# Taking two heads in one transpose: a regrouped second batch in an attention and feed-forward kernel

## The chip, the cores and the metric

One core of one Trainium2 chip runs the whole program. The metric is the device time of one execution in microseconds (us). Executions of one kernel differ by about 1%, so a kernel is given as the median of several runs with the lowest and the highest, and two kernels are compared by a ratio with a 95% interval. A run over 1.5% above the fastest of its kernel is called slow and left out of the ratio (five runs of the kernel before in all the rounds below, none of another). TensorE is the matmul engine, VectorE, ScalarE and GpSimd the others.

## The reference

```python
# q, k, v: (8 batches, 12 heads, 448 positions, 64); the weights: 768 x 1536 twice, 1536 x 768
scores = q @ k.T / sqrt(64)
attn   = relu(scores) ** 2 / 448
x      = (attn @ v)                    # regrouped to 3584 x 768
out    = (gelu(x @ w_gate) * (x @ w_val)) @ w_out
```

## The kernel before

A planner in Python lays all instructions in order: each piece of work has a place in time, and the pieces are interleaved on TensorE by their places. Nearly every matmul uses one quarter of the array, 64 rows by 64 columns. `row` and `col` name the quarter. Four matmuls on four quarters run at the same time, and a product of full width is a pair on one half of the rows (two column halves) and a pair on the other half.

```python
def mm(o, lhsT, rhs, row, col, start, stop):
    return nc.tensor.matmul(o, lhsT, rhs, start=start, stop=stop,
                            tile_position=(P * row, P * col))          # P = 64
```

Scores need q and k with the head dimension on the partitions, so both are transposed first. A batch has three groups (`m`) of four heads. The first two batches (`EARLY = 2`) are transposed on TensorE, one head at a time; later ones by DMA, from a copy `qkr` in which VectorE has put the heads of a group side by side.

```python
def add_transposes(at, b, m, rs):          # batches 0 and 1
    def emit(i, n, c):                     # i: q (upper partitions) or k (lower)
        ...
        src = qk16[b].rearrange("p (h c d) -> p h c d", c=SC, d=D)
        for j in range(2):                 # one head each
            nc.tensor.transpose(
                t[HALF[j], n, c * P:(c + 1) * P], src[HALF[i], 2 * (2 * m + rs[n]) + j, c, :],
                ident[HALF[i], HALF[i]], tile_position=(P * i, P * j))
    ...
    both(at, zip(*ops), GS / 2 if b else 0.0)

def add_dma_transposes(b, m):              # batches 2 to 7
    wait = Op("IDLE", 2.0, lambda: None,
              [head_op[b, pr, i] for pr in (2 * m, 2 * m + 1) for i in range(2)])
    def emit_copy():
        ...
        nc.vector.tensor_copy(
            qkr[b][:, m], qk16[b].rearrange("p (h c d) -> p c h d", c=SC, d=D)[:, :, 4 * m:4 * m + 4])
```

The last line of `add_transposes` matters most below: for the second batch (b = 1, counted from 0) each small step of transposes is put half a matmul step (`GS / 2`) after the last, so a group is not one run but is spread among the other matmuls. These are the gate and value products `x @ w_gate` and `x @ w_val`, which appear in the profile as `ff<-xT,wg` and `ff<-xT,wv`.

## Time and profile before

| what | before |
|---|---|
| time, 6 runs beside the changed kernel | 432.66 us median (431.25 to 435.29) |
| profiled run, span and mean granted clock | 432.1 us, 0.993 |
| two batches in the steady part | 99.1 us |
| fetch stop at 50.9 us, half clock after it | 1.94 us, 3.41 us |
| wait for the VectorE product at 96.65 us | 1.58 us |

The prediction shows the page's head and the stretches around the dips. These two stretches ahead of the first dip are used later; the columns are the stretch, its length, then TensorE, weight loads, VectorE, ScalarE and GpSimd (busy time and count each), the granted clock, the DMA share and GB/s.

```profile
30.00:40.00 10.00, 9.59 (x244) 8.76 (x243) 5.20 (x9) 6.00 (x8) 6.00 (x8) 1.00 1.39 198
40.00:50.00 10.00, 10.00 (x244) 8.08 (x239) 6.58 (x12) 6.80 (x9) 4.92 (x7) 1.00 1.45 197
```

About 244 matmuls start in each ten microseconds, at full clock.

This is TensorE's timeline of the kernel before, in the middle of a spread group: start, duration, line and operation, and how many records the line stands for.

```profile
49.30 0.22 PE L333 MATMUL sp<-ident,qk 64*64 64x64 bf16 x4
49.35 0.35 PE L159 MATMUL ff<-xT,wv 64*64 64x448 bf16 x2
49.42 0.35 PE L159 MATMUL ff<-xT,wg 64*64 64x448 bf16 x2
49.55 0.22 PE L333 MATMUL sp<-ident,qk 64*64 64x64 bf16 x4
```

Between two sets of four small transposes stand a pair on each half of the rows, 0.07 us apart, and the next transposes come 0.13 us after the second pair. The ends of matmuls are modelled: one lasts 0.35 us here, though a new set of four starts every 0.19 us. What counts is the distance between starts. The small transposes slip in at almost no cost.

A group of the page of the kernel before: busy time, mean ns of one, then the idle time of the engine just before them and what ended most of it.

```profile
L258 DVE COPY qkr<-qk 128x1792 bf16<-128x1792 bf16 x18 | 19.4, 1080 | 3.3 <-DMA qkT<-qkr 2.3
```

The 18 copies of L258 serve the six later batches, and 2.3 us of the idle time before them is a wait for the DMA transposes that still read the buffer.

### The profile page before, as it was taken

What the parts mean: (1) busy time and instruction counts of PE and PEld (TensorE: products, weight loads), DVE (VectorE), ACT (ScalarE), POOL (GpSimd) and SP (SyncE); (2) the same over time, 40 slices, a digit from 0 to 9 for tenths busy, and PEclk for the clock granted to TensorE, in tenths of its full rate; (3) what the DMA queues carried; (4) which work ended last, traced back from release to release, by engine and by line L of the source; (5) the groups of instructions that cost most, each with busy time, mean ns of one, the idle gap of its engine ahead of it and who ended that gap; (6) DMA issues with size and microseconds to landing.
All of it is one profiled execution on the core that took longest, in us unless ns stands there. A gap on an engine that the chain in (4) does not pass through costs nothing.

```text
span 432.1 us, 19964 instructions
## 1 busy us (share of the span) xinstructions
PE 419.5 (97%) x9279; PEld 361.3 (84%) x9279; DVE 212.0 (49%) x345; ACT 224.9 (52%) x323; POOL 71.6 (17%) x117
## 2 busy tenths in 40 slices
PE   8899899989999999999999999999999999999995
PEld 4568668867899888979999978979999988977895
DVE  3866556358543675356633675346643555212200
ACT  4856554266666555565556555555546555322221
POOL 7655320023000230013200231012200000000000
PEclk9999989999999999999999999999999999999998
DMA  7999999899533899259913699258912100220024
GB/s 98 193 200 197 201 209 177 144 146 168 81 76 77 99 143 96 76 90 136 146 39 90 95 150 115 77 80 130 161 39 77 39 4 2 45 70 3 3 76 111
DMA packets 75378, 44.92 MB, mean 104 GB/s; under 512 B 36128, under 2 KB 71840, under 8 KB 75296
## 3 DMA queue, kind: packets, MB, share of 16 engines
q0 software_dynamic: 37088, 24.39, 43.7%
q1 hardware_dynamic: 37968, 19.08, 25.0%
q8 instruction: 72, 1.18, 1.1%
q10 hardware_dynamic: 240, 0.20, 0.2%
q14 instruction: 10, 0.08, 0.1%
HBM read 48.76 MB, written 11.01 MB: 138 GB/s over the span
## 4 chain that ended last, share of the span: by engine, by line
PE 89%; DMA 3%; DVE 3%; issue 1%; ACT 1%; POOL 1%; ACTq 0%; SPq 0%; DVEq 0%; POOLq 0%
PE ff L159 82%; PE sp L159 7%; DMA qkT<-qkr 2%; DMA qk<-in_k_dram 2%; DVE attnT L393 1%; DVE qkT L339 1%; ACT rl L387 1%; POOL qk L211 1%; PE sp L333 1%; DVE xT L443 0%; DVE uT L487 0%; ACT osb L538 0%; ACTq L543 0%; PE ff L333 0%; SPq L262 0%
## 5 line engine op out<-in xcount | busy, mean ns | idle before, releaser
L159 PE MATMUL ff<-xT,wg 64*64 64x448 bf16 x2304 | 219.9, 351 | 1.9 <-issue 1.9
L159 PE MATMUL ff<-xT,wv 64*64 64x448 bf16 x2304 | 219.3, 351 | 1.6 <-DVE uT L487 1.6
L387 ACT ACTIVATE rl<-sp 128x896 bf16<-128x896 f32 x168 | 152.2, 919 | 104.5 <-PE sp L159 84.1
L159 PE MATMUL ff<-wo,uT 64*64 64x384 bf16 (+1 forms) x2736 | 150.6, 320 | 0.0
L159 PEld LDWEIGHTS <-wv 64*64 64x64 bf16 x2304 | 126.6, 107 | 18.9 <-issue 3.6
L159 PEld LDWEIGHTS <-wg 64*64 64x64 bf16 x2304 | 126.7, 107 | 18.8 <-issue 3.5
L393 DVE TENSOR_TENSOR attnT<-rl 128x896 bf16<-128x896 bf16 x168 | 103.8, 622 | 75.1 <-ACT rl L387 73.4
L159 PEld LDWEIGHTS <-uT 64*64 64x64 bf16 x2736 | 127.4, 107 | 4.1
L159 PE MATMUL sp<-qkT 64*64 64x448 bf16 (+1 forms) x768 | 107.6, 329 | 0.9 <-ACT rl L387 0.9
L487 DVE TENSOR_TENSOR uT<-gel,ff 128x448 bf16<-128x448 bf16 x96 | 59.5, 620 | 74.2 <-PE ff L159 64.0
L159 PE MATMUL ff<-attnT,v 64*64 64x448 bf16 (+1 forms) x768 | 85.5, 326 | 0.4 <-DVE attnT L393 0.4
L482 ACT ACTIVATE gel<-ff 128x448 bf16<-128x448 f32 x96 | 52.1, 543 | 49.5 <-PE ff L159 48.3
L538 ACT COPY osb<-ff 128x384 f32<-128x384 f32 (+1 forms) x57 | 26.9, 471 | 49.4 <-PE ff L159 46.2
L159 PEld LDWEIGHTS <-qkT 64*64 64x64 bf16 x768 | 44.0, 107 | 8.9 <-issue 3.3
L159 PEld LDWEIGHTS <-v 64*64 64x64 bf16 x768 | 45.6, 107 | 5.0 <-issue 0.5
L443 DVE TENSOR_SCALAR xT<-ff 128x448 bf16<-128x448 f32 x48 | 29.9, 623 | 32.2 <-PE ff L159 31.5
L211 POOL DMA_DIRECT2D qk<-in_q_dram x25 | 15.5, 622 | 156.5 <-DVE uT L487 149.5
L224 POOL DMA_DIRECT2D v<-in_v_dram x44 | 27.3, 628 | 35.1 <-DVE uT L487 25.4
L211 POOL DMA_DIRECT2D qk<-in_k_dram x25 | 15.4, 615 | 39.9 <-DVE uT L487 27.7
L258 DVE COPY qkr<-qk 128x1792 bf16<-128x1792 bf16 x18 | 19.4, 1080 | 3.3 <-DMA qkT<-qkr 2.3
L333 PEld LDWEIGHTS <-qk 64*64 64x64 bf16 x336 | 8.9, 112 | 4.8 <-issue 2.3
L339 DVE COPY qkT<-ff 128x448 bf16<-128x448 bf16 (+1 forms) x8 | 3.9, 503 | 6.8 <-PE ff L333 6.8
(22 smaller groups left out, 46.1 us busy)
## 6 DMA issues: line engine op xcount, KB each, us to landing
out_dram<-osb SPq DMA_DIRECT2D x54, 192.0 KB, 2.7
v<-in_v_dram POOLq DMA_DIRECT2D x42, 128.0 KB, 6.6
qk<-in_q_dram POOLq DMA_DIRECT2D x23, 224.0 KB, 5.3
qk<-in_k_dram POOLq DMA_DIRECT2D x23, 224.0 KB, 5.4
wg<-in_moe_w_gate_dram POOLq DMA_DIRECT2D x6, 384.0 KB, 10.4
wv<-in_moe_w_val_dram POOLq DMA_DIRECT2D x6, 384.0 KB, 11.4
wo<-in_moe_w_out_dram POOLq DMA_DIRECT2D x4, 576.0 KB, 15.3
v<-in_v_dram POOLq DMA_DIRECT2D x2, 384.0 KB, 10.5
```

The source lines that it names most:

```text
L159: return nc.tensor.matmul(o, lhsT, rhs, start=start, stop=stop, tile_position=(P * row, P * col))
L211: op = load(4 * (h1 - h0) * S * D, lambda: nc.gpsimd.dma_start(tile_of().rearrange("p (h x) -> p h x", h=H)[:, h0:h1, :], src[b, h0:h1].re ...
L224: return nc.gpsimd.dma_start(v16[b][HALF[i], h0:h1, :, :], v[b, h0:h1].rearrange("h (p c) d -> p h c d", c=SC)[:, :, c0:c0 + VC, :])
L258: nc.vector.tensor_copy(qkr[b][:, m], qk16[b].rearrange("p (h c d) -> p c h d", c=SC, d=D)[:, :, 4 * m:4 * m + 4])
L333: nc.tensor.transpose(t[HALF[j], n, c * P:(c + 1) * P], src[HALF[i], 2 * (2 * m + rs[n]) + j, c, :], ident[HALF[i], HALF[i]], tile_positio ...
L339: nc.vector.tensor_copy(dst[:, rs[0]:rs[-1] + 1, :, HALF[i]], box[i].rearrange("d r (c p) -> d r c p", c=SC))
L387: nc.scalar.activation(rl[:, :, :], box[0][:, :, 0:S], AF.Relu)
L393: nc.vector.tensor_tensor(a[:, :, :], box[1][:, :, :], box[1][:, :, :], op=ALU.mult)
L443: nc.vector.tensor_scalar_mul(xT[b][:, pr, :], box[0][:, 0:S], scalar1=out_scale)
L482: nc.scalar.activation(gel[b, fc][:, :], box[0][:, 0:S], AF.Gelu)
L487: u_op[b, fc].ins = nc.vector.tensor_tensor(uT[b][:, fc, :], gel.pop((b, fc))[:, :], box[0][:, 0:S], op=ALU.mult).ins
L538: nc.scalar.copy(ob[:, cols], box[0][:, 0:N])
```

## The change

The intent is to halve the number of transposes in the second batch. VectorE first puts its heads side by side, as it does for later batches, and one transpose then takes two heads, 64 rows by 128 columns of the array. Besides, the second pair of heads of the first group of batch 0 is transposed later, the first group of the second batch is placed 3 us of planned time later, fillers stop at 30 us of planned time instead of 64, and from batch 3 on the planned copy waits 5.0 us instead of 2.0 after its loads.

```diff
-    FILL = 64.0
+    FILL = 30.0
...
-    def add_dma_transposes(b, m):
+    def add_relayout(b, m):
-        wait = Op("IDLE", 2.0, lambda: None,
+        wait = Op("IDLE", 2.0 if b <= EARLY else 5.0, lambda: None,
...
+        copy = Op("DVE", 0.65, emit_copy, [wait, *tr_op.get((b - 1, m), ())], lag=0.15, prio=3)
+        DVE.append(copy)
+        return copy
...
             t = box[i]
+            if b:
+                nc.tensor.transpose(
+                    t[:, n, c * P:(c + 1) * P],
+                    qkr[b][HALF[i], m, c, 2 * rs[n]:2 * rs[n] + 2, :].rearrange("p h d -> p (h d)"),
+                    ident[HALF[i], HALF[i]], tile_position=(P * i, 0))
+                return
...
+        copy = add_relayout(b, m) if b else None
         for i in range(2):
-            have = [*(head_op[b, 2 * m + r, i] for r in rs), *(units[-SB:1 - SB] if b else ring_dep())]
+            have = [*(head_op[b, 2 * m + r, i] for r in rs), copy, *(units[-SB:1 - SB] if b else ring_dep())]
...
+            tr_op[b, m] = [ops[0][-1], ops[1][-1]]
...
-                    work.append((lo + SC * m * step - (5.0 if b else 3.0), 1, add_transposes, (b, m, rs)))
+                    x = 1.5 * step if rs == (1,) else (-5.0 if m else -2.0) if b else -3.0
+                    work.append((lo + SC * m * step + x, 1, add_transposes, (b, m, rs)))
```

More of the change, by code (lines that the diff above doesn't have):

```diff
@@ L259, in emit_copy, with add_dma_transposes @@
                 qkr[b][:, m], qk16[b].rearrange("p (h c d) -> p c h d", c=SC, d=D)[:, :, 4 * m:4 * m + 4])
+        copy = Op("DVE", 0.65, emit_copy, [wait, *tr_op.get((b - 1, m), ())], lag=0.15, prio=3)
+        DVE.append(copy)
+        return copy
+    def add_dma_transposes(b, m):
         def emit_transpose(c0, c1):
@@ L264, in emit_transpose @@
                 qkr[b][:, m, c0:c1].rearrange("p c h d -> p (c h d)"))
-        copy = Op("DVE", 0.65, emit_copy, [wait, *tr_op.get((b - 1, m), ())], lag=0.15, prio=3)
-        DVE.append(copy)
+        copy = add_relayout(b, m)
         tr_op[b, m] = [Op("SP", 0.19 * 2 * (c1 - c0), lambda c0=c0, c1=c1: emit_transpose(c0, c1),
```

## The prediction

> **What bounds the kernel now.** I read the page first.
>
> ```profile
> span 432.1 us, 19964 instructions
> ...
> PE 419.5 (97%) x9279; PEld 361.3 (84%) x9279; DVE 212.0 (49%) x345; ACT 224.9 (52%) x323; POOL 71.6 (17%) x117
> ...
> q8 instruction: 72, 1.18, 1.1%
> ```
>
> TensorE is busy for 97% of the span, every other engine for about half, so only what TensorE waits for or executes counts. Then I read busy time by stretch, over the whole span and again around each dip.
>
> ```profile
> 50.00:60.00 10.00, 7.68 (x144) 4.81 (x138) 4.44 (x9) 3.85 (x6) 2.48 (x5) 0.83 1.22 208
> 60.00:70.00 10.00, 10.00 (x227) 7.75 (x222) 6.71 (x12) 7.10 (x10) 1.64 (x3) 1.00 1.23 206
> ...
> 90.00:100.00 10.00, 8.42 (x187) 6.65 (x183) 6.58 (x10) 5.69 (x9) 1.83 (x3) 1.00 0.88 127
> ...
> 130.00:180.00 50.00, 50.00 (x1117) 44.09 (x1114) 27.03 (x44) 29.00 (x41) 7.33 (x12) 1.00 0.79 98
> ```
>
> The columns are length, then TensorE, weight loads, VectorE, ScalarE, GpSimd, granted clock, DMA share, GB/s. From 100 us to 380 us TensorE is busy 10 of 10 at full clock; the change has nothing to win there. Before that, after the start-up of 28 us (where ScalarE and VectorE take turns and TensorE runs fillers), there are just two dips: near 51 us, with a lowered clock, and near 95 us.
>
> ```profile
> 50.90:52.80 1.90, 0.00 (x0) 0.00 (x0) 0.00 (x0) 0.25 (x1) 0.61 (x1) 1.00 1.34 203
> 52.80:54.10 1.30, 1.01 (x20) 0.43 (x21) 0.57 (x1) 0.61 (x1) 0.02 (x1) 1.00 1.18 209
> 54.10:57.50 3.40, 3.29 (x38) 2.02 (x41) 1.83 (x4) 1.06 (x2) 1.20 (x2) 0.50 1.16 211
> ```
>
> The first dip: 1.94 us with no TensorE instruction, 0.4 us waiting for a copy, then 3.4 us at a clock of 0.50, which costs 3.4 x 0.5 = 1.7 us more. Together 4.0 us. In time order:
>
> ```profile
> 50.49 0.11 PEld L159 LDWEIGHTS <-wv 64*64 64x64 bf16 x2
> 50.52 0.36 PE L159 MATMUL ff<-xT,wv 64*64 64x448 bf16 x2
> ...
> 52.81 0.11 PEld L159 LDWEIGHTS <-wg 64*64 64x64 bf16 x2 [2.21 <-issue]
> 52.81 0.38 PE L159 MATMUL ff<-xT,wg 64*64 64x448 bf16 x2 [1.94 <-issue]
> ```
>
> "issue" means that nothing the profile shows held TensorE: VectorE had been idle since 50.78. I think it ran out of instructions. The instruction queue moved 72 packets, 1.18 MB, so 16 KB each; TensorE has 2 x 9279 rows, about 72 packets of 256. Putting the queue's DMA records beside TensorE's records, a fetch starts some time after TensorE enters a block of 256 and must land before it ends. The row after the stop is row 1985 = 193 + 7 x 256, on a boundary. That fetch started at 50.35, 3.7 us after TensorE entered the block at 46.62, and landed at 51.30; TensorE went on 1.51 us later. Four blocks between 16 and 47 us show similar times from landing to the next block (1.40 to 1.64), and 4.6 to 4.8 us from entry to landing in four of the five between 22 and 57. So while the weights stream in (DMA share above 1.2), 256 instructions can't be had faster than every 4.7 + 1.45 = 6.1 us. A block of full-width matmuls takes that anyway (0.189 us per 8 rows, 32 x 0.189 = 6.05). The block at 46.62 held 48 of the short transposes and only 4 us of work.
>
> The second dip:
>
> ```profile
> 94.99 1.08 DVE L258 COPY qkr<-qk 128x1792 bf16<-128x1792 bf16 x1 [2.26 <-DMA qkT<-qkr]
> ...
> 95.99 0.61 DVE L487 TENSOR_TENSOR uT<-gel,ff 128x448 bf16<-128x448 bf16 x1
> ...
> 96.65 0.38 PE L159 MATMUL ff<-xT,wv 64*64 64x448 bf16 x4 [1.58 <-DVE uT L487]
> ```
>
> VectorE reached the first regrouping copy of batch 3, whose single buffer was still being read by the last DMA transpose of batch 2, and the product behind it, which frees TensorE's bank, came late: 1.58 us lost.
>
> **What the Trainium skill says.** "Runtime: NRT & Kernel Launch", Instruction fetch mechanics, has blocks of 16 KiB (256 instructions), the next fetched while the current runs; the trace agrees on size, but not that it is hidden. "DMA: Bandwidth & Descriptors", Queues, rings and completion order, has each DMA engine go round the rows at packet granularity, which fits a fetch delayed 3.7 us at 203 GB/s. "TensorE: Matmul & The Clock Gate", What's actually happening, halves the clock after an idle window of about 3.4 us; here 1.94 us (2.3 us of the ten) was followed by 3.4 us at half clock, while the 1.11 us stop before 11.88 was not. "TensorEngine Tiling (Array Packing)", Key Properties: "Mode switching requires drain". The trace agrees for one switch, 64x64 to 128x128 and back:
>
> ```profile
> 9.41 0.39 PE L159 MATMUL sp<-qkT 64*64 64x224 bf16 x8
> 9.73 0.50 PE L296 MATMUL ff<-warm 128*128 128x256 bf16 x3
> 10.17 0.38 PE L159 MATMUL sp<-qkT 64*64 64x448 bf16 x4
> 10.49 0.28 PE L296 MATMUL ff<-warm 128*128 128x256 bf16 x1
> ```
>
> Three fillers span 0.50 us and one lasts 0.28, so they are 0.11 apart and the last starts at 9.95; the score follows 0.22 later instead of 0.11. The next switch, scores to filler, takes 10.49 - 10.17 = 0.32 where two steps of scores overlap by 0.19. Each switch costs about 0.1 us. That drain is the danger in this change.
>
> **The change part by part.** The order of both programs shows the rest.
>
> 1. Transposes of batch 1: 168 of 64x64 become 84 of 64x128, 168 TensorE rows fewer (7 more fillers, 154 fewer in all). Between neighbours' starts, dense small ones took 0.013 to 0.019 us each, 0.7 to 0.9 us per group of 56. If the big ones stream alike, 3 x 0.4 = 1.2 us are saved.
> 2. Block boundaries shift. Counting at 0.0473 us per full matmul (0.189 / 4), the blocks after the start hold 5.6, 5.4, 5.6, 5.2 and 5.9 us of work: every one is near 6.1, so instead of one stop of 1.94 I expect stops of 0.4 to 0.9, too short to lower the clock. From 30 us: 36.1, 42, 48.1, 54.2, then 102 rows (2.35 us) to the place that TensorE passed at 60.7 before: 56.5. Gain 4.2 us (3.7 to 4.6).
> 3. Three more VectorE copies, 3 x 1.08 = 3.2 us. The later two lie in idle time of VectorE, and their loads land (32.4 and 39.8 us by the semaphores) before the copies' turns near 34.7 and 41.9. The first stands before the fifth xT copy, at about 26.9, but two qkT copies (0.6 each) move behind it: xT is as early as before. Cost about 0.
> 4. Batch 0's first scores precede the second pair's transposes: 0.1 to 0.2 us of a ScalarE-bound start.
> 5. Regrouping from batch 3 on stands one gate-value step (about 2.5 us) later on VectorE, and the last batch 2 transposes are queued partly ahead of the output stores. The 1.58 us go. Later batches have no TensorE idle time to lose or win.
>
> Without a drain: 4.2 + 1.6 + 0.1 = 5.9 us, 431.3 - 5.9 = 425.4.
>
> **The rivals.** (a) 64x128 is another tiling mode than 64x64, and the new transposes stand among 64x64 matmuls in 38 separate runs: 38 x 2 x 0.1 = 7.6 us of drains, of which about 1 us is hidden in the first group, which waits for xT anyway. Blocks grow to 6.7, 7.5, 6.1 and 8.0 us, the fetch stops vanish, and the same place comes at 61.7: 1.0 us lost there, 1.6 won at 95 us, so about 430.7. For it: fillers do drain. Against it: rows stay split in the same halves, only columns merge. (b) Half a drain each (0.05): about 428. (c) Fetches stay late and one stop exceeds 2 us, so that the clock falls again: 2 us lost from the best case, 427.5. (d) The new first copy delays xT and the score behind it: up to 1 us, 426.4.
>
> **Range and chances.** I give 0.4 to no drain, 0.35 to a full one, 0.25 to between: 0.4 x 425.4 + 0.35 x 430.7 + 0.25 x 428 = 427.9; I say 427.5. 2% faster needs 422.7, more than the two dips together, so 0.05. Slower by 2% (439.9) would need drains twice as costly: 0.02.
>
> **What would show it.** Transposes from qkr: their starts to the next 64x64 matmul at about 0.03 us (no drain) or 0.1 and more (drain). The stop near 51 us: gone or below 1 us, clock 1.00 there. Around 90 to 95 us: no wait of TensorE for uT, no wait of the regrouping copy for the DMA transpose. From 100 us on: 10 of 10, the same 99.1 us per two batches. I am wrong if the steady part changes, if a stop of 2 us stays, or if the start-up before 28 us moves by over 1 us.

## The result

| | before | after |
|---|---|---|
| median of 6 runs | 432.66 us (431.25 to 435.29) | 446.61 us (442.79 to 447.71) |
| profiled run: span, mean granted clock | 432.1 us, 0.993 | 445.9 us, 0.975 |

The ratio is 1.0295, with a 95% interval of 1.0238 to 1.0352. A ratio here is the mean time of one kernel's fast runs over that of the other's fast runs of the same rounds, so it is not quite the ratio of the medians. The changed kernel is slower, and the prediction of 427.5 us, faster than before, was wrong.

The head of the page of the changed kernel, with the clock in tenths of full speed for 40 slices of 11.1 us:

```profile
span 445.9 us, 19815 instructions
...
PE 438.2 (98%) x9202; PEld 361.2 (81%) x9202; DVE 215.0 (48%) x348; ACT 225.0 (50%) x323; POOL 71.6 (16%) x117
...
PEclk9988598999999999999999999999999999999999
```

TensorE executes 77 matmuls fewer and is "busy" 18.7 us longer. The clock line says where to look: the third to seventh slices. The same stretches as before:

```profile
30.00:40.00 10.00, 9.78 (x125) 5.02 (x127) 4.14 (x7) 2.89 (x5) 5.95 (x8) 0.66 1.40 198
40.00:50.00 10.00, 10.00 (x100) 4.06 (x96) 3.06 (x6) 3.10 (x4) 4.90 (x8) 0.73 1.45 197
50.00:60.00 10.00, 10.00 (x164) 5.90 (x164) 6.63 (x11) 4.65 (x6) 2.67 (x5) 0.75 1.21 209
60.00:70.00 10.00, 10.00 (x128) 5.00 (x124) 3.81 (x7) 3.73 (x5) 1.50 (x2) 0.93 1.24 204
...
90.00:100.00 10.00, 10.00 (x229) 8.64 (x223) 2.24 (x3) 2.45 (x5) 0.62 (x1) 1.00 1.16 153
130.00:180.00 50.00, 50.00 (x1126) 44.54 (x1121) 27.14 (x44) 29.70 (x42) 7.32 (x12) 1.00 0.66 95
```

Read the counts, not the busy time. From 40 to 50 us TensorE is busy 10.00 of 10.00 in both kernels, but 100 matmuls start instead of 244, and the weight loads are busy 4.06 us instead of 8.08. A busy stretch is an unbroken chain of matmul durations here, and it says nothing of how much of the array works. The granted clock is 0.66 to 0.93 in these stretches. From 90 us on the clock is full and the counts are those of full work.

One of the stretches at half clock by itself, in the view of stretches of the changed kernel:

```profile
44.68:54.92 10.24, 10.24 (x95) 4.36 (x97) 4.03 (x6) 2.92 (x4) 4.76 (x7) 0.50 1.36 201
```

There are three such stretches: 31.03 to 37.86 (6.83 us), 44.68 to 54.92 (10.24) and 68.58 to 71.99 (3.41), which is 20.48 us in all. At half speed they lose 20.48 x 0.5 = 10.24 us. Before there was one of 3.41 us, which lost 1.71. So 10.24 - 1.71 = 8.5 us of the loss is clock alone.

To see the rest I counted only the matmuls that both kernels share (no transposes, no fillers), took the n-th of each, and subtracted the clock's loss so far. The changed kernel is then behind as follows:

| part of the program (time before, us) | behind without the clock, us | step |
|---|---|---|
| start to 27 | about 0 | |
| first group of transposes, to 29 | 1.7 | +1.7 |
| second group, to 37 | 4.8 | +3.1 |
| third group, most of it, to 50 | 7.6 | +2.8 |
| rest of the third group, past the fetch stop of before, 60 to 93 | 6.2 | -1.4 (+0.9 and -2.3) |
| past the wait of before at 96.65 | 4.5 | -1.7 |
| past small fetch stops of after, from 116 on | 5.3 | +0.8 |

The sum is 5.3 + 8.5 = 13.8 us, which is the difference between the two traces from 130 us to the end (13.78 to 13.84).

What a group looks like now, in the timeline of the changed kernel:

```profile
30.16 0.38 PE L159 MATMUL ff<-xT,wg 64*64 64x448 bf16 x2
30.47 0.29 PE L336 MATMUL sp<-ident,qkr 64*128 64x64 bf16 x6
30.69 0.38 PE L159 MATMUL ff<-xT,wg 64*64 64x448 bf16 x2
31.00 0.34 PE L336 MATMUL sp<-ident,qkr 64*128 64x64 bf16 x5
31.27 0.58 PE L159 MATMUL ff<-xT,wg 64*64 64x448 bf16 x2
```

A pair of 64x64 matmuls starts at 30.16, and the next transpose only 0.31 us later, although the pair streams its 448 columns in 0.19 us. After a single transpose the next pair starts 0.13 us later (30.03 to 30.16 just ahead of these lines). Between two sets of transposes there is now only one pair, on one half of the rows: the other half has nothing. The last duration, 0.58 us, is already at half clock.

What the prediction had expected of VectorE did happen. The group of regrouping copies, and the whole list of TensorE's waits from 20 to 100 us, in the changed kernel:

```profile
L258 DVE COPY qkr<-qk 128x1792 bf16<-128x1792 bf16 x21 | 22.6, 1078 | 0.0
```

```profile
PE sp L159 <- ACT rl L399: 0.6, 2, 0.4
PE sp L336 <- DVE qkT L349: 0.2, 1, 0.2
```

In the kernel before that list was headed by these two:

```profile
PE ff L159 <- issue: 1.9, 1, 1.9
PE ff L159 <- DVE uT L487: 1.6, 1, 1.6
```

The columns are the total, the number and the longest. Both dips are gone. A list of waits does not show the new loss at all, since it is time in which TensorE counts as busy.

### The profile page after: what moved, and what is told of

Its sections match the earlier page's. It is cut to its first block, busy times and chain, and to the rows that moved or that the text cites. A ratio compares the mean times of both kernels' runs of the same rounds, so it can differ in the third digit from the quotient of the medians.

```text
span 445.9 us, 19815 instructions
## 1 busy us (share of the span) xinstructions
PE 438.2 (98%) x9202; PEld 361.2 (81%) x9202; DVE 215.0 (48%) x348; ACT 225.0 (50%) x323; POOL 71.6 (16%) x117
## 4 chain that ended last, share of the span: by engine, by line
PE 93%; DVE 2%; DMA 1%; ACT 1%; POOL 1%; issue 1%; ACTq 0%; POOLq 0%
PE ff L159 84%; PE sp L159 7%; PE sp L336 2%; DMA qk<-in_k_dram 1%; DVE attnT L405 1%; ACT rl L399 1%; POOL qk L211 1%; DVE qkT L349 0%; DVE xT L455 0%; ACT osb L550 0%; DVE qkr L258 0%; ACTq L555 0%; PE ff L343 0%; PE ff L300 0%; POOL ident masks.py:199 0%
## 5 line engine op out<-in xcount | busy, mean ns | idle before, releaser
L159 PE MATMUL ff<-xT,wg 64*64 64x448 bf16 x2304 | 229.5, 357 | 0.3 <-issue 0.3
L159 PE MATMUL ff<-xT,wv 64*64 64x448 bf16 x2304 | 225.8, 356 | 0.0
L159 PEld LDWEIGHTS <-uT 64*64 64x64 bf16 x2736 | 126.1, 107 | 4.4
L159 PE MATMUL sp<-qkT 64*64 64x448 bf16 (+1 forms) x768 | 109.1, 335 | 0.9 <-ACT rl L399 0.9
L258 DVE COPY qkr<-qk 128x1792 bf16<-128x1792 bf16 x21 | 22.6, 1078 | 0.0
L336 PEld LDWEIGHTS <-qkr 64*128 64x128 bf16 x84 | 4.6, 98 | 11.6 <-issue 11.0
L349 DVE COPY qkT<-sp 128x896 bf16<-128x896 bf16 x6 | 3.7, 624 | 12.3 <-PE sp L336 12.3
```

What stands on the lines that cost most here:

```text
L258: nc.vector.tensor_copy(qkr[b][:, m], qk16[b].rearrange("p (h c d) -> p c h d", c=SC, d=D)[:, :, 4 * m:4 * m + 4])
L336: nc.tensor.transpose(t[:, n, c * P:(c + 1) * P], qkr[b][HALF[i], m, c, 2 * rs[n]:2 * rs[n] + 2, :].rearrange("p h d -> p (h d)"), ident[H ...
L349: nc.vector.tensor_copy(dst[:, rs[0]:rs[-1] + 1, :, HALF[i]], box[i].rearrange("d r (c p) -> d r c p", c=SC))
```

## The experiments

The theory after the result has two parts. The first: 64x128 transposes spread one by one among 64x64 matmuls cost about 0.3 us for each run of them, because the array changes its mode twice and because only one half of the rows works between. The second: the low use of the array then makes the clock fall to half. Rivals: the regrouping copies delay everything; the longer wait does; or transposes of 128 columns are slow in themselves.

### The changed kernel with small transposes

```diff
-                nc.tensor.transpose(
-                    t[:, n, c * P:(c + 1) * P],
-                    qkr[b][HALF[i], m, c, 2 * rs[n]:2 * rs[n] + 2, :].rearrange("p h d -> p (h d)"),
-                    ident[HALF[i], HALF[i]], tile_position=(P * i, 0))
+                for j in range(2):
+                    nc.tensor.transpose(
+                        t[HALF[j], n, c * P:(c + 1) * P], qkr[b][HALF[i], m, c, 2 * rs[n] + j, :],
+                        ident[HALF[i], HALF[i]], tile_position=(P * i, P * j))
```

> The changed kernel with its transposes as two of 64x64 again (same source, same copies, same 38 places among the other matmuls). Theory 1 (switches of tile mode): the loss goes altogether, no half-clock stretch after a group of transposes, 428 to 433 us; the instruction-fetch stop near 50 us comes back, since the rows are back (a block with about 4.4 us of work against 6.1 us). Rival A (the copy on VectorE and its later transposes hold TensorE up): stays at 440 to 447 us.

Measured: 432.75 us (431.15 to 434.12), ratio 0.9991 [0.9967, 1.0016]. The copies, the longer wait and the places are those of the changed kernel. Only the form of the transposes differs, and the loss of 3% is gone. The clock is 1.00 all through this trace up to the end, and the fetch stop is back. TensorE's longest wait from 20 to 100 us:

```profile
PE sp L337 <- issue: 1.8, 1, 1.8
```

So the rivals that blame the copies or the wait fall: together with their gains they come out even. What is left is the 64x128 form or its place.

### The longer wait alone

```diff
-        wait = Op("IDLE", 2.0, lambda: None,
+        wait = Op("IDLE", 2.0 if b <= EARLY else 5.0, lambda: None,
```

> The kernel before with only the later place of the regrouping copies from batch 3 on. If the step on the second dip is right: the 1.58 us wait near 95 us goes and nothing else moves, 1.3 to 1.7 us faster than before. Rival: the bank is late for another reason and nothing changes (within 0.3 us).

Measured: 431.62 us (430.07 to 433.29), ratio 0.9978 [0.9959, 0.9996], with before at 432.72. The medians differ by 1.1 us, and in the trace 1.7 us are won between 93 and 97 us. But a size can't be read from one trace. The kernel with dummies (below) executes the same instructions as the kernel before until its first dummy at 189 us, with the short wait, and in its trace the dip is gone too: the regrouping copy finds its buffer free. In the trace of the kernel with moved boundaries (below), also with the short wait, it is there again. The copy in these two traces:

```profile
90.61 1.08 DVE L258 COPY qkr<-qk 128x1792 bf16<-128x1792 bf16 x1
92.62 1.09 DVE L258 COPY qkr<-qk 128x1792 bf16<-128x1792 bf16 x1 [1.97 <-DMA qkT<-qkr]
```

So with the short wait TensorE waited in two traces of three (1.6 and 1.3 us) and with the long one in none of seven. The mechanism of that part of the prediction held; that the dip comes in every execution does not, and the 1.1 us between the medians are the better measure of what the longer wait wins.

This trace also has a fetch stop like that of before (1.9 us, at 52 us), but no half clock after it. The clock is granted in windows of 3.41 us (all the stretches above are multiples of that); in this run the stop fell across two windows, and the share of the array in use, worked out from the columns streamed, was 0.40 in the lower of the two. In the trace of before one window held nearly the whole stop, at a share of 0.21. So the 1.7 us of clock at the first dip are there by chance, in some executions only.

### Each group's wide transposes in one run

```diff
+        def emit_all():
+            for n in range(len(rs)):
+                for c in range(SC):
+                    for i in range(2):
+                        emit(i, n, c)
...
+            if b:
+                ops[i].append(Op(f"PE{i}", 0.7, emit_all if i == 0 else lambda: None, have, lag=0.2))
```

> The changed kernel with the 28 transposes of 64x128 of each group in one run: 3 runs instead of 38, 6 switches instead of 76. Theory 1: 28 x 0.03 = 0.8 us and two switches for each group, the clock stays full, 422 to 428 us, faster than both kernels. Rival B (transposes of 64x128 are slow by themselves): 436 us or more.

Measured: 430.96 us (429.29 to 434.77), ratio 0.9968 [0.9948, 0.9989]. There are now three runs of 28 instead of 38 spread ones. The same 84 wide transposes with the same data are here even a little faster than the kernel before (the longer wait alone accounts for about 1.1 us of the 1.8 between the medians), so transposes of 128 columns are not slow in themselves: what costs is how often they alternate with 64x64 matmuls. The clock stays at 1.00, also from 40 to 50 us:

```profile
40.00:50.00 10.00, 9.96 (x224) 8.14 (x214) 7.18 (x12) 6.70 (x9) 4.85 (x7) 1.00 1.46 198
```

The size was missed: 422 to 428 were expected. From 37 to 79 us each block of 256 instructions takes 5.92 to 6.20 us. A block of full-width matmuls takes nearly that by its own work (6.05 us in the prediction), but the next instructions landed only 1.24 to 1.62 us before their block began, as at the stop of before (1.51). I take this for the pace of instruction fetch, so that there was no more to win than about one stop. TensorE also waits 1.2 us once for the copy to qkT, which can't begin before a whole run is done.

### Wide and small dummies in the steady part

Dummy matmuls on zeroes were added to the kernel before: in batch 3, 22 of 64x128 one at a time within a gate and a value product; in batch 4, 44 of 64x64 at the same places; in batch 5, 24 of 64x128 far apart; in batch 6, 24 of 64x128 in one run. They write a part of the bank that nobody reads, so the result stays correct.

```diff
+                if r == 0 and fc == 4 and b in (3, 4) and (j or dc):
+                    ins = extra(b == 3)
+            if r == 0 and b == 5 and fc < 6 and dc % 3 == 0:
+                ins = extra(True)
+            if r == 0 and b == 6 and fc == 4 and g == 0 and dc == 0:
+                ins = extra(True, 24)
...
+        def extra(wide, n=1):
+            for _ in range(n):
+                for j in range(1 if wide else 2):
+                    rows = slice(0, 2 * P) if wide else HALF[j]
+                    ins = nc.tensor.matmul(box[0][rows, S:512], warm[HALF[0], rows], warm[HALF[0], 0:P],
+                                           start=False, stop=False, tile_position=(0, P * j))
```

> The kernel before with extra dummy matmuls (zeros into unused PSUM columns; the result stays right) in its steady part, in four places: 22 or so wide ones (64x128) one at a time among one batch's gate and value matmuls; the same places with two 64x64 each; 24 wide ones one at a time spread over six times as many matmuls; 24 wide ones in one run. Theory 1: dense 22 x 0.3 = 6 to 7 us and then a half-clock window or more (array use in the window below about 0.4), small ones under 1 us, spread ones 24 x 0.25 = 6 us and no half clock, one run under 1.2 us. Rival B: the one run costs as much as the dense place.

Measured, one look: 448.62 us, correct. By the shared matmuls again, set against the trace of before:

| place | delay, us | for each, us |
|---|---|---|
| 22 wide, one at a time, dense | 9.1, of which 1.7 clock | 0.336 |
| 44 small, same places | 0.55 | 0.0125 |
| 24 wide, far apart | 6.7, no half clock | 0.28 |
| 24 wide in one run | 1.04 | 0.043 |

The timeline in the dense place:

```profile
192.10 0.20 PE L490 MATMUL ff<-warm 64*128 64x64 bf16 x1
192.23 0.37 PE L159 MATMUL ff<-xT,wg 64*64 64x448 bf16 x1
192.54 0.20 PE L490 MATMUL ff<-warm 64*128 64x64 bf16 x1
192.67 0.38 PE L159 MATMUL ff<-xT,wv 64*64 64x448 bf16 x2
192.68 0.37 PE L159 MATMUL ff<-xT,wg 64*64 64x448 bf16 x1
192.98 0.20 PE L490 MATMUL ff<-warm 64*128 64x64 bf16 x1
```

From dummy to matmul it takes 0.13 us and from matmul to dummy 0.31, so the period is 0.44, whether one matmul stands between or three. That is two on average, worth 0.095 us when all four quarters are fed (four take 0.189). So each alternation costs 0.44 - 0.095 = 0.34 us, in three parts: the drain before the dummy, 0.31 - 0.19 = 0.12; the drain after it, 0.13; and 0.19 - 0.095 = 0.095, because half of the array on average stands idle while the matmuls stream. Nothing else of the change is in this kernel, and the cost is the same. This is the result that settles the direct cost. The three parts are a reading of distances; no run separates them. Behind a dummy that follows the second column half, the kernel puts matmuls on the other half of the rows, which share no quarter with it, and they too start 0.13 us later. So the wait is not for a quarter to come free.

The clock followed. The last stretch of the dense place and the one after it:

```profile
194.60:198.01 3.41, 3.41 (x25) 1.50 (x24) 2.15 (x3) 0.74 (x1) 0.61 (x1) 1.00 0.26 29
198.01:201.43 3.42, 3.42 (x38) 2.13 (x39) 0.00 (x0) 0.54 (x1) 0.00 (x0) 0.50 1.00 177
```

The dense place spans two windows, with shares of the array of 0.31 and 0.25. Only the second was followed by half clock. In the changed kernel the windows before each fall had 0.33, 0.27 and 0.33. Counted over all ten traces, from the first rise of the clock on, eight windows at full clock lay under 0.40. Seven of them (0.21 to 0.38) were followed by half clock and one, the 0.31 here, was not; no window at 0.40 or above was. So the border is not sharp. In the place with dummies far apart the share was 0.64 to 0.79, and the clock held.

### Full width: q and k of two heads in one 128x128 transpose

One run for each group as above, but each transpose takes both halves of the partitions, so there are 14 in a group, and the copies to qkT go by pairs of heads.

```diff
+                if i == 0:
+                    nc.tensor.transpose(
+                        full[:, n, c * 2 * P:(c + 1) * 2 * P],
+                        qkr[b][:, m, c, 2 * rs[n]:2 * rs[n] + 2, :].rearrange("p h d -> p (h d)"),
+                        ident[:, :])
```

> The changed kernel with q and k of two heads in one 128x128 transpose (42 instead of 84, the regrouped source makes it possible), each group's 14 in one run. If rows are what the stage up to 80 us pays for (instruction fetch, about 6 us for every 256 rows while the weights load), 86 rows fewer than the one-run kernel with 64x128 are worth up to 2 us: 429 to 431 us. If they aren't: the same as that kernel, 431. Rival: a full-size transpose drains more and loses 1 us or more.

Measured: 430.37 us (429.03 to 432.41), ratio 0.9946 [0.9924, 0.9968], with before at 432.94 in these rounds. This is 0.5% faster than the kernel before, part of it by the longer wait. The fetch stop is gone: in every block from 34 to 71 us the next block's instructions landed 2.36 us or more before they were needed. One small gap, 0.44 us between starts, is left at the boundary at 76.72 us. What it pays shows in the list of TensorE's waits from 20 to 100 us:

```profile
PE sp L159 <- DVE qkT L359: 1.2, 1, 1.2
```

In the traced execution a chance window at half clock (20.84 to 24.25 us, after one at a share of 0.38 in the start-up) cost 1.7 us more. Without the clock, the first group is passed 1.06 us later than in the kernel before, 0.28 of which stood there already at 25 us. (The next expectation says 1.26; the count gave 1.06 when redone by the times of the profile.)

### Small transposes in one run

```diff
-                    qkr[b][HALF[i], m, c, 2 * rs[n]:2 * rs[n] + 2, :].rearrange("p h d -> p (h d)"),
+                    qkr[b][HALF[i], m, c, 2 * rs[n] + j, :],
...                                        # with the one run of the third experiment
```

> The changed kernel with 64x64 transposes, each group's 56 in one run. Tells the form apart from the number of rows: by the fetch theory 168 rows more than the one-run kernel with 64x128, two stops (blocks with 4.1 and 4.0 us of work) of 1 to 2 us, 432 to 434 us. By the theory of tile modes alone (no fetch limit): 430 to 431 us, two switches a group less.

Measured: 433.34 us (431.71 to 435.04), ratio 1.0008 [0.9989, 1.0028], as the theory of fetch expected. Without any change of mode the groups in one run win nothing: a run of 56 small transposes empties a block of 256 instructions quickly, and stops of 0.9 and 2.2 us, from start to start, end at block boundaries (41.70 and 54.10 us). The window with the second stop had a share of 0.30 and was followed by half clock, which cost this execution (434.86 us, one of the slower ones) 1.7 us more. So fetch is what the number of instructions pays for in this stage.

### The kernel before with its block boundaries moved

The warm-up matmuls were cut into four times as many shorter ones, which adds 120 TensorE rows ahead of everything and moves all later boundaries against the work.

```diff
-        for _ in range(10):
+        for _ in range(40):
             for j in range(2):
-                nc.tensor.matmul(t[HALF[j], :], warm[:, HALF[j]], warm[:, :],
+                nc.tensor.matmul(t[HALF[j], 0:128], warm[:, HALF[j]], warm[:, 0:128],
```

> The kernel before with its warm-up cut into four times as many, four times shorter matmuls: the same streaming time, 120 rows more ahead of everything, so all later blocks of 256 rows begin at other matmuls. Fetch theory: the 1.9 us stop at the row where it was goes; stops stand at block boundaries again, about 0.7 us near 51 us and 1.3 us near 57 us. Rival (that matmul waits for something of its own): 1.9 us before the same matmul.

Measured, one look: 431.87 us. The stop of 1.9 us is replaced by stops of 0.73, 0.71 and 1.04 us at the new boundaries, where about 0.7 and 1.3 were expected for the latter two. The stop belongs to the boundary, and not to the work that happened to stand there.

### Full width, but the first group small

The first of the regrouping copies stands before the first products. Does it cost the time lost there?

```diff
+        wide = b and m
...
-            if b:
-                if i == 0:
+            if wide:
+                if i == 0:
...
-        copy = add_relayout(b, m) if b else None
+        copy = add_relayout(b, m) if wide else None
```

> The kernel with 128x128 transposes in one run per group, but the first group of the second batch transposed as in the kernel before (56 transposes of 64x64 straight from the loaded tile, among the matmuls, with no regrouping copy); the other two groups stay in one run. Theory A, the first regrouping copy costs the second batch about 1.2 us, since it stands before the first products: about 429.2 us, ratio to before 0.992, and in the trace the matmul that ends the first group comes 1.2 us earlier than with all three groups in one run. Theory B, the first group's 1.26 us comes from the run of transposes waiting for a score bank and from its own copies to qkT, or the time is taken back later by the instruction fetch, since a group of small transposes brings more instructions per us of work: 430 to 431 us, with a fetch stop of 0.5 us or more between 30 and 60 us.

Measured: 430.26 us (429.17 to 433.44), ratio 0.9935 [0.9902, 0.9969], with before at 432.52. That is no faster than the full width in all three groups. In the trace the first group is passed 0.78 us later than before, instead of 1.06. But the traces already differ at 25 us, ahead of the group, by up to 1 us either way, so the growth from 25 to 35 us is the better measure: it is 0.78 us with full width in all groups and -0.17 here. With the regrouping copies it is 0.4 to 0.5 us in the runs with small transposes (spread and in one run) and with 64x128 in one run; in the run with the longer wait alone it is 0. So the first copy and the places that go with it cost something between 0.4 and 0.95 us, which one trace for each kernel can't narrow. Then a fetch stop of 1.09 us, from start to start, ends at 79.51 us, as theory B said it might, though it fell later than the 30 to 60 us that it named.

## Why the prediction was wrong

**What bounds the kernel** was read rightly: the steady part did not move (99.1 us for two batches in both), the start-up before 27 us moved by 0.08 us between these two traces (by luck, since the others lie from 0.9 us ahead to 1.1 us behind there), and the whole difference arises between 27 and about 116 us.

**Step 2, the fetch stop, right in mechanism.** The stop comes back with the small transposes, and it moves with the block boundary. That it is gone in the changed kernel proves nothing of the step's new boundaries: blocks there take 6.3 to 12.8 us between 33 and 73 us because TensorE is slow, and fetch is no limit any more, as rival (a) had it. The stops of 0.4 to 0.9 us that the step expected were not there to be seen. Its worth was overrated: of the 4.0 us of the first dip, the 1.7 us of clock are chance, since the run with the longer wait alone had the same stop without them.

**Step 5, the second dip, right in mechanism, its size partly chance.** The wait of 1.58 us is gone, and no trace with the longer wait has it. But an execution with the short wait did without it too, and the longer wait alone won 1.1 us in the median.

**Steps 3 and 4, right for xT, else not settled.** The first copy started at 26.86 us, as the prediction had it (about 26.9), and the fifth copy to xT behind it at 27.89, earlier than the 28.28 of before. The sixth came later, at 30.14 against 29.36, but VectorE did not hold it up; it waited for TensorE's product:

```profile
30.14 0.62 DVE L455 TENSOR_SCALAR xT<-ff 128x448 bf16<-128x448 f32 x1 [1.63 <-PE ff L159]
```

The growth of 0.4 us and more in the first group with regrouping copies (last experiment) is a cost all the same, of the order of rival (d). The price of step 4 was not tested apart.

**Step 1 and rival (a) are what failed.** Step 1 let the wide transposes "stream alike" and counted 1.2 us of gain. Rival (a) saw the drain, in 38 runs with two switches each, and had 0.1 us for a switch. The drain measured 0.12 to 0.13, so that size was nearly right, and the chance of 0.35 was too low. But its sum for the loss had two terms missing:

- Between two runs only one row half has work, because a single pair of matmuls separates them. That adds 0.095 us to each, so an alternation costs 0.34 us at full clock, not 0.2. At half clock the timeline has 0.51 us from pair to transpose (32.26 to 32.77) and 0.17 back, so 0.68; half of it counts as clock, and 0.34 - 0.095 = 0.24 is left. Nine of the 38 runs stand at half clock, so the mean is 0.32 and 38 runs are an estimate of 12.0 us, from which the 2.4 us that the small transposes had taken (3 groups of about 0.8, by the prediction's reading of before) are saved: 9.6 us. The three groups measured 1.7 + 3.1 + 2.8 + 0.9 = 8.5 us. That also holds some delay of the first copy, and some of the first group is hidden behind its wait for xT.
- The clock. The rival made TensorE slower but left its clock at 1.00, even though the prediction had the half clock after the first dip in front of it. It looked for stops with no instruction. Here no stop exceeded 0.4 us, but the array was used at about 0.3 for several windows, and that was enough. This term is 10.24 us, the largest of all, and no step of the prediction has it. At half clock the alternations also take longer, so the next window is low too: the fall in the second group lasted three windows.

Rival (a) ended at 430.7 us (from 431.3 for the kernel before, which measured 432.66 beside the changed one). Put the 10.24 us of clock on it, and 38 x 0.095 = 3.6 us for the idle half, and it comes to 444.5, an estimate near the measured 446.6.

**The chances.** Slower by over 2% got 0.02, on the ground that it "would need drains twice as costly". They did not have to be: its cases, from 425.4 to 430.7 us, left out what a low use of the array can do to the clock.

**What stays open.** The use of the array below which the clock fell here lies at about 0.4, in windows of 3.41 us, but one window at 0.31 did not lower it, and why is not known. Nor was it traced why the six runs of the changed kernel fall in two sets, 442.8 and 442.9 us against 446.4 to 447.7. Their mean clocks (0.987 against 0.973 to 0.976) fit fewer windows at half clock, which is argued and not shown.

## What to carry to other kernels

Count how often TensorE changes its tiling, not how many instructions a wider tiling saves: each lone 64x128 instruction among 64x64 ones cost about 0.3 us here, while 24 of them in one run cost 0.04 each. After any change that thins out TensorE's work, read the number of matmuls and the granted clock of each stretch, since "busy 10 of 10" stood over an array that did less than half the work. If a wider transpose is wanted, give it one run for each group. The two versions that take the full width as well have the lowest ratios here (0.9946 and 0.9935, against 0.9968 for 64x128 in one run), though the intervals overlap; part of each gain is the longer wait, and the rest I put down to fewer instructions to fetch. Before a dip is put on account, look whether a second execution of the same kernel has it.

## What the Trainium skill lacked or had wrong

- "TensorE: Matmul & The Clock Gate", What's actually happening: its table has the half clock after an idle window. Here windows in which TensorE never stood still for over 0.4 us, with about 0.3 of the array in use, were followed by half clock (three times in the changed kernel, once after the dense dummies). The page also tells, under A second HAM failure mode, of short idle times between groups of matmuls that make the clock swing; it gives no share of use at which that begins (0.21 to 0.38 here). The window of 3.41 us agrees.
- "TensorEngine Tiling (Array Packing)", Key Properties: the drain at a change of mode is right, but no size is given. Between 64x64 and 64x128 it took 0.12 us one way and 0.13 us the other at full clock, and a lone 64x128 instruction cost 0.28 to 0.34 us in all.
- No page says what the fetch of instructions costs beside heavy loads; "Runtime: NRT & Kernel Launch", Instruction fetch mechanics, has it mostly hidden. At about 200 GB/s of loads seven blocks of 256 TensorE instructions in a row took 5.92 to 6.20 us each, with the next one landing 1.24 to 1.62 us before its turn (third experiment), and the stops at boundaries were 0.6 to 2.3 us from start to start.
